# Fillers, halved first weights and a split last product in a recurrent attention and gated FFN kernel

## The chip, the cores and the metric

The kernel runs on one core of a Trainium2 chip. The metric is device time in microseconds (us) of that core, from several executions; lower is better. One further execution was taken by the hardware profiler; its lines are quoted below. In them PE is the matrix engine (PEld its weight loads), DVE the vector engine, ACT the scalar engine, POOL the general engine, and SP the engine that here only issues DMAs. "SPq", "ACTq" and the like are an engine's instruction queue, where DMAs are issued. L394 is line 394 of the kernel.

## The reference

One transformer layer, 2048 tokens of width 640, in bf16. Attention has 32 heads of 128 and is recurrent: it goes through the tokens in 64 segments of 32, and each segment sees 8 memory tokens that are the previous segment's attention output.

```python
for s in range(n_seg):                               # 64 segments, one after the other
    h = concatenate([mem, x[:, s*32:(s+1)*32]])      # 8 memory tokens and 32 tokens
    q, k, v = h @ Wq, h @ Wk, h @ Wv                 # 640 -> 32 heads of 128
    p = softmax(where(mask, q @ k.T * scale, -1e9))
    o = (p @ v) @ Wo                                 # back to 640
    mem = o[:, :8]                                   # what the next segment waits for
    outs.append(o[:, 8:])
```

x is layer-normalized before attention; h = x + attention. After it, for all 2048 tokens: `h2 = h + ((relu(g) * u) @ W_down)` with `g = ln(h) @ W_gate`, `u = ln(h) @ W_up` and 1728 hidden columns.

## The kernel before

The program is written as one list of operations, each with an engine, what it reads and what it writes. `_Graph.solve` turns the keys into semaphore waits, and each engine then runs its operations strictly in the order of the list. DMAs are operations of the engine that issues them (`dma`, L332, on SP unless `eng="act"`); SP's and ACT's DMAs go through two queues. Nothing reorders the list, so the place of a line in the source is its place on its engine.

The work has three stages.

- **Opening** (to about 57 us). SP issues the weights in one row: Wk, Wq and Wv in five pieces of 128 rows each (1 MB a piece, `W[:, j, c, :]`), then Wo in eight pieces. ACT issues two pieces of x (`xt`, `x0`, which borrows the tile oTe) and the first memory (`wtok`). DVE and ACT normalize x, PE transposes it (L360), and then PE makes K and Q of segment 0, of the tokens that are kept for memory use and of the extra tokens (`project`, L394 and L367, three passes per piece). V follows piece by piece (`first_values`). `scores` (L483), exponentials on ACT, masks on DVE, the P·V products (`pv_mem`, L536) and the products with Wo (`wo_pairs`, L599, and `wo_pass`, L582) follow, until `to_act_split` writes the memory rows of segment 1. `keep_busy(n, cols)` (L895) issues 4n products into a bank whose content is not used; it stands in places where PE would otherwise wait.
- **Segments 1 to 63** (to about 826 us). In a loop, PE projects K, Q and V of one segment, and the scores, the P·V products and the products with Wo follow. V is copied into a second layout, VM, by SP's DMAs (`merge_v`); in segment 0 DVE and ACT do this. Toward the end, SP also loads what the FFN needs: `xn2T`, the normalized tokens of the first FFN block, in segment 62, and the gate, up and down weights (`load_piece`, `load_down`).
- **FFN**. Four blocks of 512 tokens: `gate_up` (L858, with the rest of the hidden columns in L871), then `down_pair`: `down_part` multiplies 14 pieces of the hidden columns with W_down into two banks of 320 output columns, `down_out` (DVE, L1133) adds h, `down_store` writes the rows. The very last 128 tokens are done half by half: 14 products of 320 columns, an add, a store, and the same for the other 320 columns.

PE's program is far larger than what the core holds at once: it comes in 16 KB packets through an instruction queue on the same DMA engines (page: 200 packets, 3.28 MB).

Of the kernel before, what the change touches and what calls it, by code (L numbers as in the profile page):

```python
# [27 lines left out]
class _Graph:  # L28
# [10 lines left out]
    def add(self, eng, fn, r=(), w=(), dma=False):  # L39
        if eng == "pool" and not dma:  # L40
            r, w = tuple(r) + (("pool",),), tuple(w) + (("pool",),)
        op = _Op(eng, fn, tuple(r), tuple(w), dma)
        self.ops.append(op)
        return op
# [122 lines left out]
def build_kernel(nc, A_x, A_mem0, A_Wq, A_Wk, A_Wv, A_Wo, A_seg_len, B_W_gate, B_W_up, B_W_down, out):  # L167
# [110 lines left out]
    def B(n):  # L278
        return ("B", n)
# [4 lines left out]
    add("pool", lambda p: p.affine_select(ident[:], ident[:], [[1, 128]], ALU.is_equal, 0.0, base=0,  # L284
                                          channel_multiplier=-1), r=[("ident",)], w=[("ident",)])
    add("pool", lambda p: p.memset(eps[:], 1e-5), w=[("eps",)])
    for i in range(2):
        add("dve", lambda v, i=i: v.memset(oT[i][:], 0.0), w=[("oT", i, n, kh) for n in "mx" for kh in range(2)])
        add("pool", lambda p, i=i: p.memset(act_r[i][:], 0.0),
            w=[("act", i, j, "m") for j in range(4)] + [("act", i, "x")] + [("act", i, "x", j) for j in range(4)])  # L290
        if i == 0:
            add("pool", lambda p: p.memset(ap(Vp, Dh, [[VW, 8], [1, VW - Dh]]), 1.0), w=[("Vp1",)])
        add("pool", lambda p, i=i: p.memset(ap(Ve[i], Dh, [[VW, 8], [1, VW - Dh]]), 1.0), w=[("Ve1", i)])
        add("pool", lambda p, i=i: p.memset(act_e[i][:], 0.0), w=[("acte", i)])
# [30 lines left out]
    def table(a):  # L325
        return a.add_instruction(mybir.InstLoadActFuncSet(name=nc.get_next_instruction_name(), ins=[], outs=[],
                                                          act_func_set_id=6))
    add("act", table)


    def dma(dst, src, r=(), w=(), eng="sp"):
        add(eng, lambda e: e.dma_start(dst, src), r=r, w=w, dma=True)  # L332
# [40 lines left out]
    def project(act, akeys, j, halves, banks, chunks=range(5), ends=(0, DC - 1), held=False, parts=0):  # L373
        swap = 1 if j == 2 and akeys[0][0] == "acte" else 0

        def f(pe):
            left = parts
            for c in chunks:
                for n, i in enumerate(halves):
                    for g in range(4):  # L380
                        o = 2048 * i
                        w = (W[:, j, c, o + 512 * (g ^ swap):o + 512 * (g ^ swap) + 512] if j == 2 else
                             W[:, j, c, o:o + 2048].rearrange("p (h e) -> p h e", e=128)[:, :, 32 * g:32 * g + 32])
                        a = (bank(banks[n])[32 * g:32 * g + 32, :], act[:, c, :], w)
                        if n == 0 and not (held and c == chunks[0]):
                            k = min(left, 2) if c != ends[0] else 0
                            left -= k
                            for q in range(2 if k else 1):
                                b = a if not k else (a[0][:, 256 * q:256 * q + 256], a[1],
                                                     w[:, 256 * q:256 * q + 256] if j == 2 else w[:, 8 * q:8 * q + 8])  # L390
                                if q and k == 1:
                                    ins = again(pe, *b, c == ends[0], c == ends[1], g)
                                else:
                                    ins = pe.matmul(*b, start=(c == ends[0]), stop=(c == ends[1]), skip_group_check=True)  # L394
                        else:
                            ins = again(pe, *a, c == ends[0], c == ends[1], g)
            return ins
        add("pe", f, r=list(akeys) + [("W", j, c) for c in chunks], w=[B(b) for b in banks] + [("Wdone", j)])

    def tok_keys(t):  # L400
        return [("tok", t)] + [("ox", kh, t) for kh in range(2) if t < 2]
# [323 lines left out]


    x0 = oTe[:].rearrange("p h t -> p (h t)")[:, 0:D]
    ln1_load(-1, xt, ("xt",), "act")
    ln1_load(0, x0, ("oTe", 0), "act")
    for g in range(4):  # L730
        dma(wtok[32 * g:32 * g + M, :, :],
            mem0_ap.rearrange("t (c g j) -> g t c j", g=4, j=32)[g], r=[("wtok",)], w=[("wtok0", g)], eng="act")
    srcs = (A_Wq, A_Wk, A_Wv)
    for j in (1, 0, 2):
        for c in range(DC):
            dma(W[:, j, c, :], srcs[j][128 * c:128 * c + 128].rearrange("p h e -> p (h e)"), w=[("W", j, c)])
    for i, lo, hi in [(i, g, g + 1) for i in range(2) for g in range(4)]:
        dma(ap(Wo, (4 * i + 8 * lo) * D, [[8 * D, hi - lo], [1, 4 * D]]),
            A_Wo[16 * i + 4 * lo:16 * i + 4 * hi].rearrange("(g c) (p f) d -> (c p) g (f d)", c=4, f=4), w=[("Wo", i, lo)])
# [159 lines left out]

    scores(0, 0)  # L900
    scores(0, 1)
    first_values((3,))
    keep_busy(20, 32)
    first_values((4,))
    for hf in range(2):
        exp_mem(0, hf)
        mask_mem(0, hf)
# [11 lines left out]
    for a, eng in ((0, "dve"), (1, "act")):  # L919
        (t, ks), flat = v_of(0, a), "p k d -> p (k d)"  # L920
        for x, lo, hi in ((0, 0, 1), (1, 1, 3), (0, 3, 4)):
            x ^= a
            for q in range(lo, hi):
                for k0, k1 in ((0, 4), (4, 8)) if eng == "dve" else ((0, 8),):
                    copy_op(eng, VM[x][32 * q:32 * q + 32, k0:k1].rearrange(flat),
                            t[32 * q:32 * q + 32, k0:k1].rearrange(flat), ks, [("VM", x, q)])
    late_q(1, [("oT", 0, "m", 1)])
    project(xe, xke, 2, (0, 1), BQ, (0, 1))
    for g in range(4):
# [25 lines left out]
    for s in range(1, NSEG):  # L955
# [16 lines left out]
        if s > 0:  # L972
# [29 lines left out]
            else:  # L1002
                norm_x_late(0)
                flip_ox(s - 1, (0,))
            if s == NSEG - 2:
                for n, (lo, hi) in enumerate(((0, 1), (1, 2), (2, 3), (3, DC))):
                    dma(xn2T[0][:, lo:hi, :], xn2_d[:, lo:hi, :], r=[("xn2_d", u) for u in range(4)] + [("Wdone", 0)],
                        w=[("xn2", 0, n)])
            project(a, ks, 2, (0,), (P2,), range(4), held=not last and held[2])
            scores(s, 0, (0, 1))  # L1010
            project(a, ks, 2, (0,), (P2,), (4,))
# [1 line left out]
            if not last:  # L1013
                exp_mem(s, 0)
                first_exp = G.ops[-1]
                mask_mem(s, 0)
            to_v(P2, Vp, 0, ("Vp",), "act")
            if last:
# [80 lines left out]
                r=[("act", p, "x", j), ("act", p, "x"), ("act", *place(s + 1), "m")], w=[("acte", 1 - p)])  # L1099


    def down_part(par, u, bks, js, hfs=(0, 1)):

        def f(pe):
            for j in js:
                p0, p1 = (0, 128) if j < FC - 1 else ((FR, 128) if u % 2 == 0 else (0, FR))
                for hf in hfs:
                    a = (bank(bks[hf])[:, 0:320], hT[par][p0:p1, j, u * 128:(u + 1) * 128],
                         Wd[p0:p1, j, hf * 320:(hf + 1) * 320])
                    if hf == hfs[0] or j == FC - 1:  # L1110
                        i = pe.matmul(*a, start=(j == 0), stop=(j == FC - 1), skip_group_check=True)  # L1111
                    else:
                        i = again(pe, *a, j == 0, j == FC - 1, None)
            return i
        wk = sorted({n for j in js for n in ((j // 3,) if j < FC - 1 else (5, 6))})
        add("pe", f, r=[("hT", par, j) for j in js] + [("Wd", n) for n in wk], w=[B(bks[hf]) for hf in hfs])

    def down_tails(par, u0, bks):

# [9 lines left out]

    def down_out(par, u, bks, o, hfs=(0, 1)):  # L1130
        for hf in hfs:
            bk = bks[hf]
            add("dve", lambda v, hf=hf, bk=bk: v.tensor_tensor(osb[o][:, hf * 320:(hf + 1) * 320], bank(bk)[:, 0:320],  # L1133
                                                               h_rows[par][:, u, hf * 320:(hf + 1) * 320], ALU.add),
                r=[B(bk), ("h", par, u)], w=[("osb", o, hf)])

    def down_store(b, u, o, hfs=(0, 1)):
        t0 = b * TB + u * 128
        lo, hi = 320 * hfs[0], 320 * hfs[-1] + 320
        dma(out_ap[t0:t0 + 128, lo:hi], osb[o][:, lo:hi], r=[("osb", o, hf) for hf in hfs], w=[("out", t0, hfs[0])])  # L1140

    def down_pair(b, n):
        par = b % 2
        s0 = 4 * (par ^ 1 ^ n)
        bks = ((s0, s0 + 1), (s0 + 2, s0 + 3))
        u = 2 * n
        o = [(n_o[0] + q) % 3 for q in range(2)]
        n_o[0] += 2
        final = b == NBLK - 1 and n == 1
        for js in (range(FC - 2), range(FC - 2, FC if final else FC - 1)):  # L1150
            down_part(par, u, bks[0], js)
        if final:
            down_out(par, u, bks[0], o[0])
            down_store(b, u, o[0])
            for hf in range(2):
                down_part(par, u + 1, bks[1], range(FC), (hf,))
                down_out(par, u + 1, bks[1], o[1], (hf,))
                down_store(b, u + 1, o[1], (hf,))
            return
        down_part(par, u + 1, bks[1], range(FC - 1))  # L1160
        down_tails(par, u, bks)
        for q in range(2):
            down_out(par, u + q, bks[q], o[q])
            down_store(b, u + q, o[q])
# [143 lines left out]
```

## Time and profile before

| | |
|---|---|
| median of the runs | 1000.89 us (1000.19, 1000.89, 3407.01) |
| profiled execution | 1000.27 us, span 998.5 us |
| PE, busy share of the span | 97% |
| DVE, ACT, POOL | 72%, 53%, 17% |
| mean granted PE clock | 0.998 |
| DMA, mean over the span | 73 GB/s |
| DMA, 7 to 20 us | 417 GB/s |

The span runs from the first to the last instruction of the profiled execution; the 1.8 us between it and that execution's time lie around it. "Busy" counts instructions in flight, and products overlap, so a busy PE is not PE at its peak. The granted clock is the share of the full PE clock that the chip allowed. A chain of waits follows the work back from the last instruction: at each step to what released it, or to the instruction before it on its engine. A wait for several things is put down to the one that came last.

### The profile page before, as it was taken

Reading aid. Unit: us, or ns where it says so; the run is one execution under the profiler, and the core shown is the slowest. Engines: PE = TensorE matmul, PEld = TensorE weight load, DVE = VectorE, ACT = ScalarE, POOL = GpSimd, SP = SyncE. Lnnn points to the kernel's source line nnn. Section 1 sums busy time; section 2 is a strip of 40 time slices with the busy share of each in tenths; the row PEclk is TensorE's granted clock in tenths of the full one; section 3 lists DMA queues with packets and bytes.
Section 4 is the critical chain, followed back from the end, with each engine's and each line's share of the span. In section 5 each row is a group of like instructions: output and inputs, shape, how many; then the busy total and the mean of one; then the engine's idle time right before and its main releaser. Section 6 shows DMA issues by size and latency. Waiting matters only on the chain.

```text
span 998.5 us, 56385 instructions
## 1 busy us (share of the span) xinstructions
PE 970.3 (97%) x26139; PEld 534.8 (54%) x24878; DVE 715.3 (72%) x1866; ACT 524.4 (53%) x1330; POOL 167.7 (17%) x414
## 2 busy tenths in 40 slices
PE   4789999999999999999999999999999999999998
PEld 1245555555555555555556565655555554344443
DVE  2468787878888887888788878787878766445332
ACT  1456666656666666666666566665656643122120
POOL 7021202021302130222022212121110010000000
PEclk9999999999999999999999999999999999999999
DMA  9930212121222122121212131111111169413100
GB/s 376 415 108 28 54 28 54 30 60 51 54 42 54 48 55 47 48 55 48 50 45 62 46 60 41 41 41 39 41 36 39 36 183 248 99 20 93 27 14 26
DMA packets 73535, 73.34 MB, mean 73 GB/s; under 512 B 42352, under 2 KB 60112, under 8 KB 71376
## 3 DMA queue, kind: packets, MB, share of 16 engines
q1 hardware_dynamic: 71568, 68.83, 24.6%
q8 instruction: 200, 3.28, 1.4%
q10 hardware_dynamic: 1728, 0.91, 0.3%
q14 instruction: 39, 0.32, 0.1%
HBM read 37.04 MB, written 6.55 MB: 44 GB/s over the span
## 4 chain that ended last, share of the span: by engine, by line
PE 93%; SPq 3%; DMA 2%; DVE 1%; ACT 0%; issue 0%; DVEq 0%; ACTq 0%
PE ps L394 47%; PE ps L858 11%; PE ps L367 7%; PE ps L582 7%; PE ps L599 7%; PE ps L642 4%; SPq L332 3%; PE ps L1111 3%; PE ps L483 2%; PE ps L671 2%; DMA Wo<-in_A_Wo_dram 2%; PE ps L536 2%; PE ps L871 0%; PE ps L1124 0%; DVE oT L562 0%
## 5 line engine op out<-in xcount | busy, mean ns | idle before, releaser
L394 PE MATMUL ps<-W,act_r 128*32 128x512 bf16 (+1 forms) x8327 | 453.6, 357 | 1.4 <-DVE act_r L623 0.8
L394 PEld LDWEIGHTS ps<-W,act_r 128*32 128x32 bf16 x8327 | 213.4, 96 | 165.6 <-DVE act_r L623 31.9
L418 ACT ACTIVATE tok<-ps 128x512 bf16<-128x512 f32 x190 | 109.3, 594 | 57.2 <-PE ps L394 48.7
L394 PE MATMUL ps<-W,act_e 128*32 128x512 bf16 x1224 | 119.8, 384 | 7.6 <-DVE TBf L464 3.8
L413 DVE STREAM_TRANSPOSE Ko<-tox 128x512 bf16<-128x512 bf16 x128 | 89.6, 701 | 40.4 <-ACT tox L418 40.1
L491 POOL COPY Qo<-Qe 128x256 bf16<-128x256 bf16 x64 | 28.2, 440 | 527.3 <-DVE oT L556 520.3
L418 ACT ACTIVATE tox<-ps 128x512 bf16<-128x512 f32 x134 | 79.6, 598 | 63.6 <-PE ps L394 43.0
L562 DVE STREAM_TRANSPOSE oT<-tox 128x512 bf16<-128x512 bf16 x128 | 96.6, 755 | 0.0
L413 DVE STREAM_TRANSPOSE Qo<-tok 128x512 bf16<-128x512 bf16 x124 | 85.7, 691 | 0.8
L367 PE MATMUL ps<-W,act_e 128*32 128x512 bf16 x856 | 84.4, 385 | 0.0
L582 PE MATMUL ps<-Wo,oT 128*32 128x160 bf16 x4032 | 81.6, 233 | 1.0 <-DMA Wo<-in_A_Wo_dram 0.9
L599 PE MATMUL ps<-Wo,oT 128*32 128x320 bf16 x2016 | 79.8, 299 | 0.5 <-DVE rm L546 0.5
L582 PEld LDWEIGHTS ps<-Wo,oT 128*32 128x32 bf16 x4032 | 70.5, 97 | 11.1 <-DVE oT L556 3.1
L418 ACT ACTIVATE Vp<-ps 128x512 bf16<-128x512 f32 x127 | 75.2, 592 | 0.5 <-PE ps L858 0.5
L886 ACT ACTIVATE g<-ps 128x512 bf16<-128x512 f32 x52 | 30.1, 593 | 79.3 <-PE ps L858 79.3
L612 ACT ACTIVATE SA<-TA 64x40 f32<-64x40 f32 x126 | 29.5, 234 | 75.3 <-DVE TA L610 74.5
L499 ACT ACTIVATE Pm<-ps 128x64 bf16<-128x64 f32 x126 | 28.1, 223 | 71.8 <-PE ps L483 71.7
L887 DVE TENSOR_TENSOR hT<-g,ps 128x512 bf16<-128x512 bf16 x52 | 35.8, 688 | 40.5 <-PE ps L858 38.6
L858 PE MATMUL ps<-xn2T,Wg 128*128 128x512 bf16 x260 | 64.7, 379 | 0.0
L858 PE MATMUL ps<-xn2T,Wu 128*128 128x512 bf16 x260 | 64.6, 379 | 0.0
L599 PEld LDWEIGHTS ps<-Wo,oT 128*32 128x32 bf16 x2016 | 52.9, 96 | 15.8 <-DVE rm L546 1.2
L556 DVE STREAM_TRANSPOSE oT<-om 128x128 bf16<-128x128 bf16 x126 | 39.0, 309 | 31.0 <-ACT om L548 31.0
(113 smaller groups left out, 1444.5 us busy)
## 6 DMA issues: line engine op xcount, KB each, us to landing
VM<-Vp SPq DMA_DIRECT2D x126, 65.0 KB
VM<-Vp SPq DMA_DIRECT2D x63, 130.0 KB
W<-in_A_Wk_dram SPq DMA_DIRECT2D x5, 1024.0 KB
W<-in_A_Wq_dram SPq DMA_DIRECT2D x5, 1024.0 KB
W<-in_A_Wv_dram SPq DMA_DIRECT2D x5, 1024.0 KB
Wo<-in_A_Wo_dram SPq DMA_DIRECT2D x8, 640.0 KB
attn_d<-wtok SPq DMA_DIRECT2D x248, 7.5 KB
xt<-in_A_x_dram SPq DMA_DIRECT2D x16, 160.0 KB
```

Of the source, the lines that this page charges most:

```text
L367: return pe.add_instruction(mybir.InstMatmult(name=nc.get_next_instruction_name(), engine=mybir.EngineType.PE, ins=[pe.lower_ap(rhs), pe.l ...
L394: ins = pe.matmul(*b, start=(c == ends[0]), stop=(c == ends[1]), skip_group_check=True)
L413: add("dve", lambda v: v.transpose(dst[:, 16 * i:16 * i + 16, 0:32], tok[t][:, :].rearrange("p (h f) -> p h f", f=32)), r=tok_keys(t), w=keys)
L418: add("act", lambda a: a.activation(dst, src, ACTF.Copy), r=r, w=w)
L556: add("dve", lambda v: v.transpose(ap(oT[par], 160 * hf, [[40, 4], [320, 4], [1, 8]]), ap(om, 128 * hf, [[1, 4], [4, 32]])), r=[("om", hf) ...
L562: add("dve", lambda v, kh=kh: v.transpose(ap(oT[p], 160 * kh + M, [[320, 4], [40, 4], [1, 32]]), ap(tox, 128 * kh, [[256, 4], [1, 4], [4, ...
L582: i = pe.matmul(bank(bk)[32 * gg:32 * gg + 32, 0:160], src[:, hb, 0:32], w[:, gg], start=(hb == CH[16 * halves[0]]), stop=(hb == CH[-1]), ...
L599: i = pe.matmul(bank(bk)[32 * q:32 * q + 32, 0:320], src[:, hb, 0:32], w, start=(n == 0), stop=(n == 7), skip_group_check=True)
L642: ins = pe.matmul(bank(bk)[32 * q:32 * q + 32, 0:320], src[:, hb, 0:32], w[:, 2 * (q % 2):2 * (q % 2) + 2], start=(i == 0), stop=(i == 15) ...
L858: ins = pe.matmul(bank(bk), w[:, c, lo:lo + 128], xn2T[par][:, c, :], start=(c == 0), stop=(c == DC - 1))
L886: add("act", lambda a: a.activation(g1[gi][:, :], bank(bg), ACTF.Relu), r=[B(bg)], w=[("g1", gi)])
L887: add("dve", lambda v: v.tensor_tensor(hT[par][:, j, :], g1[gi][:, :], bank(bu), ALU.mult), r=[B(bu), ("g1", gi)], w=[("hT", par, j)])
```

## The change

Seven edits:

1. The tile `oT[1]` is no longer cleared at the start (DVE); `oT[0]` still is.
2. ACT's table load moves from the head of ACT's list to behind its first DMA issues.
3. The first piece of Wk (128 rows) is loaded in two halves: rows 0 to 63 by ACT, ahead of its other DMAs, rows 64 to 127 by SP. The first K products wait for both.
4. Fillers: 12 wide products (512 columns) before V's fourth piece, then 32 narrow ones (32 columns) and 20 wide ones where 80 narrow ones stood, and 16 wide ones after V's fifth piece.
5. In segment 0 DVE copies V into VM in whole rows instead of two halves.
6. The loads of `xn2T` in segment 62 move behind the first exponential of that segment, and wait for it.
7. The last 128 tokens are split into 480 and 160 output columns instead of 320 and 320.

```diff
+    add("dve", lambda v: v.memset(oT[0][:], 0.0), w=[("oT", 0, n, kh) for n in "mx" for kh in range(2)])
     for i in range(2):
-        add("dve", lambda v, i=i: v.memset(oT[i][:], 0.0), w=[("oT", i, n, kh) for n in "mx" for kh in range(2)])
...
-    add("act", table)
...
-        add("pe", f, r=list(akeys) + [("W", j, c) for c in chunks], w=[B(b) for b in banks] + [("Wdone", j)])
+        add("pe", f, r=list(akeys) + [("W", j, c) for c in chunks] + [("W", 1, 0, 0)] * (j == 1 and 0 in chunks), w=[B(b) for b in banks] + [("Wdone", j)])
...
+    dma(W[0:64, 1, 0, :], A_Wk[0:64].rearrange("p h e -> p (h e)"), w=[("W", 1, 0, 0)], eng="act")
     ln1_load(-1, xt, ("xt",), "act")
     ln1_load(0, x0, ("oTe", 0), "act")
...
+    add("act", table)
     srcs = (A_Wq, A_Wk, A_Wv)
     for j in (1, 0, 2):
         for c in range(DC):
-            dma(W[:, j, c, :], srcs[j][128 * c:128 * c + 128].rearrange("p h e -> p (h e)"), w=[("W", j, c)])
+            lo = 64 if (j, c) == (1, 0) else 0
+            dma(W[lo:, j, c, :], srcs[j][128 * c + lo:128 * c + 128].rearrange("p h e -> p (h e)"), w=[("W", j, c)])
...
     scores(0, 0)
     scores(0, 1)
+    keep_busy(3)
     first_values((3,))
-    keep_busy(20, 32)
+    keep_busy(8, 32)
+    keep_busy(5)
     first_values((4,))
+    keep_busy(4)
...
-                for k0, k1 in ((0, 4), (4, 8)) if eng == "dve" else ((0, 8),):
-                    copy_op(eng, VM[x][32 * q:32 * q + 32, k0:k1].rearrange(flat),
-                            t[32 * q:32 * q + 32, k0:k1].rearrange(flat), ks, [("VM", x, q)])
+                copy_op(eng, VM[x][32 * q:32 * q + 32].rearrange(flat), t[32 * q:32 * q + 32].rearrange(flat), ks, [("VM", x, q)])
...
-            if s == NSEG - 2:
-                for n, (lo, hi) in enumerate(((0, 1), (1, 2), (2, 3), (3, DC))):
-                    dma(xn2T[0][:, lo:hi, :], xn2_d[:, lo:hi, :], r=[("xn2_d", u) for u in range(4)] + [("Wdone", 0)],
-                        w=[("xn2", 0, n)])
             project(a, ks, 2, (0,), (P2,), range(4), held=not last and held[2])
             scores(s, 0, (0, 1))
...
                 exp_mem(s, 0)
                 first_exp = G.ops[-1]
+                if s == NSEG - 2:
+                    for n, (lo, hi) in enumerate(((0, 1), (1, 2), (2, 3), (3, DC))):
+                        dma(xn2T[0][:, lo:hi, :], xn2_d[:, lo:hi, :], r=[("xn2_d", u) for u in range(4)] + [("Wdone", 0)],
+                            w=[("xn2", 0, n)])
+                        G.ops[-1].after = first_exp
                 mask_mem(s, 0)
...
+    COLS = ((0, 320), (320, 640), (0, 480), (480, 640))
...
-                    a = (bank(bks[hf])[:, 0:320], hT[par][p0:p1, j, u * 128:(u + 1) * 128],
-                         Wd[p0:p1, j, hf * 320:(hf + 1) * 320])
+                    lo, hi = COLS[hf]
+                    a = (bank(bks[hf % 2])[:, 0:hi - lo], hT[par][p0:p1, j, u * 128:(u + 1) * 128], Wd[p0:p1, j, lo:hi])
...
-            for hf in range(2):
+            for hf in (2, 3):
                 down_part(par, u + 1, bks[1], range(FC), (hf,))
                 down_out(par, u + 1, bks[1], o[1], (hf,))
                 down_store(b, u + 1, o[1], (hf,))
```

The adds and stores of the last rows (`down_out`, `down_store`) take their columns from the same `COLS`.

More of the change, by code (lines that the diff above doesn't have):

```diff
@@ L1115, in down_part @@
         wk = sorted({n for j in js for n in ((j // 3,) if j < FC - 1 else (5, 6))})
-        add("pe", f, r=[("hT", par, j) for j in js] + [("Wd", n) for n in wk], w=[B(bks[hf]) for hf in hfs])
+        add("pe", f, r=[("hT", par, j) for j in js] + [("Wd", n) for n in wk], w=[B(bks[hf % 2]) for hf in hfs])
     def down_tails(par, u0, bks):
@@ L1131, in down_out @@
         for hf in hfs:
[L1132 to L1135, printed above, removed]
+            bk, (lo, hi) = bks[hf % 2], COLS[hf]
+            add("dve", lambda v, lo=lo, hi=hi, bk=bk: v.tensor_tensor(osb[o][:, lo:hi], bank(bk)[:, 0:hi - lo],
+                                                                      h_rows[par][:, u, lo:hi], ALU.add),
+                r=[B(bk), ("h", par, u)], w=[("osb", o, n) for n in {2: (0, 1, 2)}.get(hf, (hf,))])
     def down_store(b, u, o, hfs=(0, 1)):
         t0 = b * TB + u * 128
-        lo, hi = 320 * hfs[0], 320 * hfs[-1] + 320
+        lo, hi = COLS[hfs[0]][0], COLS[hfs[-1]][1]
         dma(out_ap[t0:t0 + 128, lo:hi], osb[o][:, lo:hi], r=[("osb", o, hf) for hf in hfs], w=[("out", t0, hfs[0])])
```

## The prediction

> **What bounds the kernel now.** I read the chain of waits first, as shares, then cut to the opening.
>
> ```profile
> PE 93%; SPq 3%; DMA 2%; DVE 1%; ACT 0%; issue 0%; DVEq 0%; ACTq 0%
> ...
> 33.26 2.13 SPq L332
> 35.43 20.14 DMA Wo<-in_A_Wo_dram
> 55.57 0.04 issue
> 55.61 0.49 PE ps L582 x16
> ```
>
> From 57 us to the end the chain is PE's, with nothing in it that the diff touches before the last products. The first 55.6 us are not PE's: the chain goes through SP's weight issues to the last piece of Wo, landed at 55.57, and the sixteen L582 products that wait for it. Second view, the stages (columns: stretch, its length, busy time of PE, PEld, DVE, ACT, POOL, granted clock, DMA share, GB/s):
>
> ```profile
> 1.80:5.00 3.20, 0.00 (x0) 0.00 (x0) 0.47 (x1) 0.29 (x1) 2.67 (x10) 1.00 0.92 331
> 5.00:20.50 15.50, 5.58 (x54) 1.58 (x34) 5.57 (x23) 0.99 (x4) 11.53 (x59) 1.00 1.02 415
> 34.20:37.60 3.40, 1.05 (x16) 0.21 (x8) 1.37 (x3) 0.11 (x1) 0.00 (x0) 1.00 1.01 419
> 37.60:41.00 3.40, 3.04 (x88) 1.32 (x80) 0.55 (x4) 0.81 (x4) 0.00 (x0) 0.50 1.01 417
> 50.00:53.60 3.60, 3.58 (x88) 1.73 (x72) 0.97 (x3) 2.85 (x6) 0.27 (x1) 1.00 1.01 405
> ```
>
> The DMA engines are full (share 1.0, 405 to 421 GB/s) from 5 us to 53.6. Only the ramp before 5 us is below that. After a stretch in which PE was busy 1.05 of 3.40 us the clock is 0.50, in 37.6 to 41.0 only. Third view, PE in order of time where fillers are changed (start, length, what, idle before it and who ended that):
>
> ```profile
> 40.39 0.62 PE L394 MATMUL ps<-W,act_e 128*32 128x512 bf16 x4
> ...
> 41.57 0.52 PE L895 MATMUL ps<-W,act_e 128*32 128x32 bf16 x48
> 43.80 0.38 PE L895 MATMUL ps<-W,act_e 128*32 128x32 bf16 x32 [1.71 <-issue]
> 44.00 0.42 PE L394 MATMUL ps<-W,act_e 128*32 128x512 bf16 x4
> ...
> 45.90 0.24 PE L536 MATMUL ps<-Ve,Pbd 128*32 128x129 bf16 x4 [0.83 <-ACT Vp L418]
> ```
>
> After 48 of 80 narrow fillers PE stands 1.71 us and nothing in the profile ends it. The DMA view of 41 to 42 us shows one 16 KB packet of the instruction queue: I take 43.80 as a border, where the next block of PE's program had to arrive through the full DMA engines.
>
> **The change, part by part.** The profiled execution took 1000.27 us (span 998.5, 1.77 around it); the median shown is 1000.89, the lowest run 1000.19. My sum is against 1000.27.
>
> First weights in halves. Bytes are the same, so only the ramp can give. SP's first issue takes 0.39 us for 128 rows. Two halves issued side by side put descriptors before all engines in about half that: I take 0.2 us. Bounds: nothing; and the whole ramp, (415-331) x 3.2 / 415 = 0.65 us. I take the lower part because only the issue is halved, not the first reads. The ACT queue now carries 0.5 MB ahead of xt, oTe and wtok: 1.3 us later at 415 GB/s, 2.5 at half of it. wtok sets PE's start (L394 waits until 17.05), so the K products start 1.3 to 2.5 us later, and may pay one more half-clock window (3.4 us of work at half pace, 1.7). PE is idle 0.94, 1.35 and 1.43 us for the three V pieces at 33.02, 35.42 and 37.91, 3.7 in all, which takes up what I expect: cost 0. Without that cover it is paid one for one. The new wait, K's first product on the second half, has all of PE behind it. That product began at 12.18, and the half is due near 5 us.
>
> Table load after the issues: six ACT issues end at 5.5 us, seven near 6.1, plus 1.28 of loading gives 7.4 against the first ACTIVATE at 7.20. 0.2 us on the x rows, which wait for wtok anyway: 0. One memset less (0.59 on DVE, which then waits 3.78 for xt): 0. Whole VM copies on DVE instead of eight halves (306 ns each, 2.4 in all; four whole ones cost between 1.2 and 2.4): DVE waits for L599 afterwards, so 0.
>
> Fillers. Count stays 80, so the border stays at the same instruction, but now 12 wide products stand before V's piece 3, then 32 narrow and some 4 wide reach the border, and 16 wide follow it; 16 more stand after piece 4. A wide one costs 54 ns (sixteen from 48.24 to 49.10), double at half clock. Piece 3 was ready at 40.39; twelve from 40.33, half of them slow, end near 41.3, so it ends near 42.2, still before the border. If the block again arrives for 43.80, 16 wide take 0.86 and piece 4 starts at 44.66 instead of 44.00: 0.66 late. The last 16 (0.86) lie under the 1.2 us before the P·V products (0.83 of it idle). So the P·V products and everything behind them come 0.66 late. Cover: PE's waits for Wo before 52.47, 54.04 and 55.61. After the preceding fillers' last issue they are 0.17, 0.63 and 0.63, 1.43 in all. Cost 0, with 0.77 left. Bounds: 0 (nothing in front of 55.61 can gain, Wo lands when it lands) and, beyond the cover, one for one; no row shows a border with another order in front.
>
> xn2T loads (L332, segment 62). Four issues, 2.04 us from 798.34, now wait for the first exp (ACT 798.96, 0.22 long), so start 0.9 us later. Behind them on SP are the three VM pieces (issued from 801.00, now about 801.3) and two weight pieces (803.23). VM is read at 807.18, four us after its last issue; xn2T and the weights at 810.02. Cost 0. Without the cover PE waits one for one.
>
> The end. Groups by shape (busy us, mean ns of one | idle before):
>
> ```profile
> L871 PE MATMUL ps<-xn2T,Wt 128*128 128x256 bf16 x40 | 5.0, 272 | 0.0
> ...
> L360 PE MATMUL ps<-ident,xt 64*128 64x64 bf16 x5 | 0.4, 235 | 8.3 <-DVE xt L350 8.3
> ...
> L627 DVE TENSOR_TENSOR fold<-ps,fold 128x160 f32<-128x160 f32 x1 | 0.3, 318 | 0.0
> ```
>
> And the last add in order of time:
>
> ```profile
> 995.43 0.49 DVE L1133 TENSOR_TENSOR osb<-ps,h 128x320 bf16<-128x320 f32 x1 [1.62 <-PE ps L1111]
> ```
>
> The chain gives 0.136 us per 320-column product, 0.217 per 512 (L858, 90 in 19.53) and 0.109 per 256 (L871, 10 in 1.09): 0.42 ns a column. 480 columns then cost 0.203 and 160 cost 0.069; 14 x (0.203+0.069) = 3.81 = 28 x 0.136. PE: 0, if loading 128 columns of weights hides under 0.069. L360 says so: five in 0.44 with 0.235 each, 0.05 apart at the cold start, weights loaded between. Bound above: no narrower product at full clock than L871's, 14 x (0.109-0.069) = 0.56. [...] The last add shrinks from 0.49 to the 0.32 of L627's 160 columns: -0.17. The store's payload halves: 40 KB less at 415 GB/s is at most 0.1, not counted.
>
> Sum: -0.2 - 0.17 = -0.37, so 999.9.
>
> **Rivals.**
>
> No gain in the opening: the two halves share the same full engines, and the stream's end is set by its slowest engine. For: the DMA share is 0.92 already in 1.8 to 5.0. Then only -0.17 is left: 1000.1. [...]
>
> Slower: PE arrives late at the last piece of Wo (55.61). It decides where the delay of V's piece 4 passes 1.43 us. If the wider fillers delay the border block too (0.98, what stands before piece 3) and the 16 wide behind it run in a half-clock window (another 0.86), the delay is 0.66+0.98+0.86 = 2.5, less 1.43 = +1.07, with the end's -0.17: 1001.2. For: the block's fetch began at 41.4, just as piece 3 was issued. Against: the border is counted in instructions, and 24 of them moved ahead of it.
>
> The narrow last pass is load-bound: 14 x 0.04 = +0.56, with the rest of the sum 1000.4.
>
> Faster: the whole ramp of 0.65 is won, with -0.17: 999.4.
>
> **How the numbers follow.** Forecast 0.40, no gain in the opening 0.25, slower 0.12, load-bound end 0.10, whole ramp 0.11, something not seen here 0.02. The likeliest gives 999.9. The range is 998.9 to 1001.2: below, the whole ramp (999.4) less half of the 0.7 between the median and the lowest run and the store's 0.1; above, the slower case, which also holds the forecast if the run falls like 1000.89. Two per cent is 20 us, about what a measurement here tells from no change; no case moves over 1.1 us, so within 0.98 and 0.01 on either side for the unseen.
>
> **What would show it.** The last Wo landing near 55.4 and the last L582 group waiting for it (right), or that group following the filler before it without a wait (slower rival). First V piece still started by its DMA. A gap behind 36 fillers after piece 3, then 16 wide, piece 4 near 44.7. Products of the last pass 0.07 apart (right) or 0.11 (load-bound). Last add near 0.32. No PE wait at 807 or 810. A time off by more than 1.1 us would mean that a cause outside these rows acts.

## The result and the profile after

| | before | after |
|---|---|---|
| median of 12 runs | 1000.89 us | 1003.38 us |
| lowest run | 1000.11 us | 1002.51 us |
| profiled execution | 1000.27 us, span 998.5 us | 1004.5 us, span 1002.5 us |
| last piece of Wo landed | 55.57 us | 57.83 us |
| last group of products that needs it | 55.61 us | 59.04 us |

After is 2.5 us slower by the medians; the ratio of the runs is 1.0028, with a 95% interval of 1.002 to 1.0036. One run of before took 3407.01 us, for a reason that nothing here shows; it does not move the median. The profiled execution of after is one of its longer ones, 4.0 us over before in span. Line numbers have moved: L394 is now L392, L367 is L365, L895 is L896, L582 is L580, L536 is L534, L1111 is L1116, L1133 is L1138, and the DMA helper L332 is L330.

First the chain of waits of the kernel after, as shares and then cut to the opening (start, length, what):

```profile
PE 94%; DMA 3%; DVE 1%; SPq 1%; issue 1%; ACT 0%; DVEq 0%; ACTq 0%
```

```profile
11.79 30.96 DMA W<-in_A_Wv_dram
42.80 0.40 PE ps L392 x4
...
44.29 2.16 issue
46.45 1.05 PE ps L896 x16
...
49.12 1.71 PE ps L896 x16
```

SP's share fell from 3% to 1%. Before, the chain stayed with the weight stream until the last piece of Wo at 55.57. Now it leaves the stream with V's fourth piece at 42.80 and goes on through PE: a stand of 2.16 us and two groups of wide fillers. So there are two things to explain: why V's fourth piece is at 42.80 instead of 40.39, and why PE is behind Wo afterwards.

For the first, the stages in the first 9 us (columns: stretch, its length, busy time of PE, PEld, DVE, ACT, POOL, granted clock, DMA share, GB/s), of before:

```profile
1.80:4.00 2.20, 0.00 (x0) 0.00 (x0) 0.47 (x1) 0.29 (x1) 1.86 (x7) 1.00 0.93 309
4.00:6.50 2.50, 0.00 (x0) 0.00 (x0) 0.45 (x2) 0.00 (x0) 1.91 (x9) 1.00 1.01 393
6.50:9.00 2.50, 0.44 (x5) 0.28 (x5) 1.26 (x6) 0.50 (x2) 1.88 (x10) 1.00 1.02 411
```

and of after:

```profile
1.80:4.00 2.20, 0.00 (x0) 0.00 (x0) 0.00 (x0) 0.00 (x0) 1.85 (x7) 1.00 0.88 238
4.00:6.50 2.50, 0.00 (x0) 0.00 (x0) 0.00 (x0) 0.00 (x0) 1.91 (x9) 1.00 1.02 220
6.50:9.00 2.50, 0.00 (x0) 0.00 (x0) 0.00 (x0) 1.28 (x1) 1.88 (x10) 1.00 0.94 254
```

The next-to-last column says that the DMA engines are nearly as busy as before. The last says that they move 56 to 77% as much. The packets of the weights are 8 KB in both; between 4 and 6.5 us their median time is 312 ns before and 602 ns after. The share of busy time alone would have hidden this: from 4 to 6.5 us a share of 1.02 went with 220 GB/s, where one of 1.01 went with 393. The halves landed one after the other, SP's at 6.07 and ACT's at 8.90; the whole piece had landed at 5.71. Every later piece of the weights landed later than before too, by 1.6 to 3.1 us, most of them by 2.3 to 2.5.

For the second, PE in order of time (start, length, what, idle before it and who ended that), after:

```profile
42.80 0.40 PE L392 MATMUL ps<-W,act_e 128*32 128x512 bf16 x4 [0.26 <-DMA W<-in_A_Wv_dram]
...
43.67 0.62 PE L896 MATMUL ps<-W,act_e 128*32 128x32 bf16 x36
46.45 1.05 PE L896 MATMUL ps<-W,act_e 128*32 128x512 bf16 x16 [2.16 <-issue]
47.33 0.51 PE L392 MATMUL ps<-W,act_e 128*32 128x512 bf16 x4
...
48.89 1.93 PE L896 MATMUL ps<-W,act_e 128*32 128x512 bf16 x16
50.60 0.34 PE L534 MATMUL ps<-Ve,Pbd 128*32 128x129 bf16 x4
...
59.04 0.46 PE L580 MATMUL ps<-Wo,oT 128*32 128x160 bf16 x16
```

and the stages around it:

```profile
44.10:47.50 3.40, 1.24 (x24) 0.44 (x20) 0.00 (x0) 0.00 (x0) 0.00 (x0) 1.00 1.03 415
47.50:50.90 3.40, 3.40 (x45) 1.33 (x36) 1.72 (x3) 1.19 (x2) 0.00 (x0) 0.50 1.02 413
```

The border stands behind 36 fillers, as forecast, but 2.16 us long. After it the granted clock is 0.50 for 3.4 us, and the second sixteen wide fillers take 1.93 us instead of 1.05. The last L580 group starts without a wait, 1.21 us after its Wo landed; before it started 0.04 us after. So at 59 us after is 3.43 us behind: 2.26 by the stream, 1.17 by PE. By the end of the segments it is 4.18: 0.33 more within the next 12 us, 0.51 more around the moved loads of segment 62, and 0.09 regained between them. The end gives 0.17 back: 4.0.

The end, in order of time:

```profile
998.32 1.10 PEld L1116 LDWEIGHTS ps<-Wd,hT 128*128 128x128 bf16 x14 [0.21 <-issue]
998.42 0.66 DVE L1138 TENSOR_TENSOR osb<-ps,h 128x480 bf16<-128x480 f32 x1 [2.15 <-PE ps L1116]
999.60 0.32 DVE L1138 TENSOR_TENSOR osb<-ps,h 128x160 bf16<-128x160 f32 x1 [0.52 <-PE ps L1116]
```

The last add takes 0.32 instead of 0.49. Fourteen weight loads of the narrow pass fit into 1.10 us, 0.08 apart, and the last thirty products take 4.61 us in the chain of waits of both kernels.

### The profile page after: what moved, and what is told of

Read it like the earlier page. It is cut to its first block, busy times and chain, and to the rows that moved or that the text cites. A ratio compares the mean times of both kernels' runs of the same rounds, so it can differ in the third digit from the quotient of the medians.

```text
span 1002.5 us, 56373 instructions
## 1 busy us (share of the span) xinstructions
PE 971.7 (97%) x26125; PEld 536.1 (53%) x24878; DVE 713.9 (71%) x1861; ACT 524.5 (52%) x1330; POOL 167.4 (17%) x414
## 4 chain that ended last, share of the span: by engine, by line
PE 94%; DMA 3%; DVE 1%; SPq 1%; issue 1%; ACT 0%; DVEq 0%; ACTq 0%
PE ps L392 47%; PE ps L859 11%; PE ps L365 7%; PE ps L580 7%; PE ps L597 7%; PE ps L640 4%; PE ps L1116 3%; DMA W<-in_A_Wv_dram 3%; PE ps L481 2%; PE ps L669 2%; PE ps L534 2%; SPq L330 1%; PE ps L896 1%; PE ps L872 0%; PE ps L1129 0%
## 5 line engine op out<-in xcount | busy, mean ns | idle before, releaser
L392 PE MATMUL ps<-W,act_r 128*32 128x512 bf16 (+1 forms) x8327 | 453.7, 357 | 2.2 <-ACT tok L416 1.2
L392 PEld LDWEIGHTS ps<-W,act_r 128*32 128x32 bf16 x8327 | 213.3, 96 | 167.4 <-DVE act_r L621 32.1
L392 PE MATMUL ps<-W,act_e 128*32 128x512 bf16 x1224 | 119.6, 383 | 3.9 <-DVE TBf L462 3.6
L365 PE MATMUL ps<-W,act_e 128*32 128x512 bf16 x856 | 84.5, 386 | 0.0
L580 PE MATMUL ps<-Wo,oT 128*32 128x160 bf16 x4032 | 81.4, 233 | 0.2 <-DVE oT L554 0.2
L580 PEld LDWEIGHTS ps<-Wo,oT 128*32 128x32 bf16 x4032 | 70.8, 97 | 9.5 <-DVE oT L554 3.5
L859 PE MATMUL ps<-xn2T,Wg 128*128 128x512 bf16 x247 | 61.8, 379 | 1.3 <-issue 1.0
L554 DVE STREAM_TRANSPOSE oT<-om 128x128 bf16<-128x128 bf16 x126 | 39.0, 309 | 31.5 <-ACT om L546 31.4
```

The costliest lines, as they stand in the source:

```text
L365: return pe.add_instruction(mybir.InstMatmult(name=nc.get_next_instruction_name(), engine=mybir.EngineType.PE, ins=[pe.lower_ap(rhs), pe.l ...
L554: add("dve", lambda v: v.transpose(ap(oT[par], 160 * hf, [[40, 4], [320, 4], [1, 8]]), ap(om, 128 * hf, [[1, 4], [4, 32]])), r=[("om", hf) ...
L580: i = pe.matmul(bank(bk)[32 * gg:32 * gg + 32, 0:160], src[:, hb, 0:32], w[:, gg], start=(hb == CH[16 * halves[0]]), stop=(hb == CH[-1]), ...
L859: ins = pe.matmul(bank(bk), w[:, c, lo:lo + 128], xn2T[par][:, c, :], start=(c == 0), stop=(c == DC - 1))
```

## The experiments

Each was timed against runs of the kernel before on the same chip (medians 1000.61 to 1000.73), unless it says one execution. "Shift" is the time after minus before, by the profiles, at which the first products with VM start (59.10 us in before), the first group behind the opening that is the same in all.

### Each suspect alone

**Edit 3 alone**, put into before:

```diff
+    dma(W[0:64, 1, 0, :], A_Wk[0:64].rearrange(...), w=[("W", 1, 0, 0)], eng="act")
...
+            lo = 64 if (j, c) == (1, 0) else 0
-            dma(W[:, j, c, :], srcs[j][128 * c:128 * c + 128]...)
+            dma(W[lo:, j, c, :], srcs[j][128 * c + lo:128 * c + 128]...)
```

> The kernel before with edit 3 alone (first Wk piece in row halves from ACT's and SP's queue). Theory 'stream': the halves move at 220 to 240 GB/s instead of 415, all later pieces land 2.2 to 2.6 us later (last Wo piece at about 57.9 instead of 55.57), and the time rises by 2.0 to 2.6 us. Rival 'fillers': the stream's loss hides under PE's waits, the time rises by under 0.7 us.

Measured: 1002.96 us, ratio 1.0023 (1.0014 to 1.0031). The stages and the last group of products:

```profile
4.00:6.50 2.50, 0.00 (x0) 0.00 (x0) 0.00 (x0) 0.00 (x0) 1.91 (x9) 1.00 0.97 210
```

```profile
58.66 0.46 PE L582 MATMUL ps<-Wo,oT 128*32 128x160 bf16 x16
```

Wo's last piece landed at 57.98. This edit alone carries the slow rate and 2.2 of the 2.5 us. Here too PE is 0.68 late at Wo, with the old fillers, in a half-clock window from 46.99 to 53.82.

**After without edit 3** (the piece in one DMA again, everything else as changed):

```diff
-    dma(W[0:64, 1, 0, :], A_Wk[0:64].rearrange(...), w=[("W", 1, 0, 0)], eng="act")
...
-            dma(W[lo:, j, c, :], srcs[j][128 * c + lo:128 * c + 128]...)
+            dma(W[:, j, c, :], srcs[j][128 * c:128 * c + 128]...)
```

> The changed kernel with edit 3 undone, all else kept. Theory 'stream': the last Wo piece lands near 55.5 again; left are +0.5 from the moved xn2T loads, -0.2 at the end and at most 0.5 from the fillers: 0 to +0.8 us against before. Rival 'fillers': most of the loss stays, +2 us or more.

Measured: 1000.36 us, ratio 0.9998 (0.9989 to 1.0007). In order of time:

```profile
44.06 1.05 PE L894 MATMUL ps<-W,act_e 128*32 128x512 bf16 x16 [1.85 <-issue]
...
55.78 0.46 PE L580 MATMUL ps<-Wo,oT 128*32 128x160 bf16 x16 [0.44 <-DMA Wo<-in_A_Wo_dram]
```

With the piece whole again, the loss is gone, and the wait for Wo is back in its old place.

**The fillers alone**, edit 4 put into before:

```diff
+    keep_busy(3)
     first_values((3,))
-    keep_busy(20, 32)
+    keep_busy(8, 32)
+    keep_busy(5)
     first_values((4,))
+    keep_busy(4)
```

> The kernel before with edit 4 alone (the fillers). Theory 'stream': V's last piece starts 0.5 to 0.8 us later, the last Wo products still wait for their DMA at 55.6, time within 0.4 us of before. Rival 'fillers': the last Wo products start without a wait, 1 to 2 us late, and the time rises by as much.

Measured: 1000.49 us, ratio 0.9997 (0.9988 to 1.0006), shift 0.0.

```profile
44.06 1.05 PE L895 MATMUL ps<-W,act_e 128*32 128x512 bf16 x16 [1.28 <-issue]
...
55.61 0.46 PE L582 MATMUL ps<-Wo,oT 128*32 128x160 bf16 x16 [0.30 <-DMA Wo<-in_A_Wo_dram]
```

The block behind the border came 0.26 later than in before (44.06 for 43.80). V's last piece started at 44.92, 0.92 later, a little more than expected (0.5 to 0.8), and the P·V products 0.91 later. All of it was taken up ahead of Wo: 0.30 of wait is left.

**After with the old fillers** (the last diff reversed):

> The changed kernel with the fillers of before. Theory 'stream': the last Wo products wait for their DMA near 57.9; time against before +2.3 to +2.9 (stream 2.3, moved loads 0.5, end -0.2), so 0 to 1.2 us below the changed kernel, whose PE came 1.2 us after the landing. Rival 'fillers': within 0.7 us of before.

Measured: 1003.13 us, ratio 1.0023 (1.0014 to 1.0033). The border takes 2.87 us here, Wo lands at 58.17, and the last L580 group starts at 58.22. So the fillers are not the cause of the loss. Against their own runs of before the two kernels lose 2.49 us with the new fillers and 2.40 with the old ones; the difference is too small to be told here.

### What about the halves is slow

**Rows 0 to 63 and 64 to 127, both from SP's queue**, in before:

```diff
-            dma(W[:, j, c, :], srcs[j][128 * c:128 * c + 128]...)
+            for lo, hi in (((0, 64), (64, 128)) if (j, c) == (1, 0) else ((0, 128),)):
+                dma(W[lo:hi, j, c, :], srcs[j][128 * c + lo:128 * c + hi]...)
```

> The kernel before, first Wk piece as two DMAs of 64 rows, both on SP's queue. Theory 'half the rows': a transfer that goes to 64 of the 128 partitions moves at half rate whatever its queue; 8 KB packets near 600 ns instead of 309 until about 6 us, last Wo piece near 57.8, time +2 us or more. Rival 'two queues': alternating between two queues is what costs; packets stay at 309 ns, time within 0.7 us of before.

Measured: 1003.1 us, ratio 1.0024 (1.0015 to 1.0033), last Wo at 57.43.

```profile
4.00:6.50 2.50, 0.00 (x0) 0.00 (x0) 0.70 (x2) 0.00 (x0) 1.91 (x9) 1.00 1.01 211
```

One queue is as slow (211 GB/s). The second queue is not the cause.

**Two halves by columns**, 128 rows of 4 KB each, from ACT and SP:

```diff
+    dma(W[:, 1, 0, 0:2048], A_Wk[0:128, 0:16].rearrange(...), w=[("W", 1, 0, 0)], eng="act")
...
+            lo = 16 if (j, c) == (1, 0) else 0
+            dma(W[:, j, c, 128 * lo:], srcs[j][128 * c:128 * c + 128, lo:]...)
```

> The kernel before, first Wk piece as two DMAs of 128 rows and half the columns each, from ACT's and SP's queue. Theory 'half the rows': full rate, last Wo piece at 55.3 to 55.9, time within 0.5 us of before, though x lands later. Rival 'two queues': as slow as row halves, last Wo near 57.9, +2 us.

Measured: 1000.94 us, ratio 1.0002 (0.9994 to 1.0011), last Wo at 55.67.

```profile
4.00:6.50 2.50, 0.00 (x0) 0.00 (x0) 0.00 (x0) 0.00 (x0) 1.91 (x9) 1.00 1.03 419
```

Halves from two queues that span all rows moved at 419 GB/s from 4 to 6.5 us (393 in before), and gained nothing.

**Even rows from ACT, odd rows from SP**, 64 rows each:

```diff
+    dma(W[0:128:2, 1, 0, :], A_Wk[0:128:2].rearrange(...), w=[("W", 1, 0, 0)], eng="act")
...
+                dma(W[1:128:2, j, c, :], srcs[j][1:128:2]...)
```

> The kernel before, first Wk piece as two DMAs of 64 rows, even rows from ACT's queue and odd rows from SP's. If one side of the partitions being idle is what costs, this spreads over both sides and runs at full rate: last Wo near 55.6, time within 0.5 us. If the number of rows (64 instead of 128) costs, or the two queues do, +2 us as with the row halves.

Measured: 1001.01 us, ratio 1.0003 (0.9994 to 1.0012), last Wo at 55.54.

```profile
4.00:6.50 2.50, 0.00 (x0) 0.00 (x0) 0.00 (x0) 0.00 (x0) 1.91 (x9) 1.00 0.95 392
```

So it is not the number of rows either: two times 64 rows, each spread over alternate partitions, moved at 392 GB/s. Its profile has a half-clock window from 44.04 to 50.87 and a shift of 0.92; the times, 0.4 us over before, neither show that much nor exclude it.

**Destination and source apart.** In the last runs the rows read and the partitions written changed together. Two kernels change only one of them; both use SP's queue. In both, Wk's first 128 rows stand in another order in W, and K is computed from that. The first reads alternate rows and writes neighbouring partitions:

```diff
+            if (j, c) == (1, 0):
+                for n in range(2):
+                    dma(W[64 * n:64 * n + 64, 1, 0, :], A_Wk[n:128:2].rearrange(...), ...)
+                continue
```

> Before, with the first Wk piece as two transfers from SP's queue: rows 0, 2, 4 .. 126 of Wk's first 128 go to partitions 0 to 63, rows 1, 3 .. 127 to partitions 64 to 127. So Wk's first 128 rows stand in another order and K is computed from that; every byte and every product is there. If the range of SBUF partitions written decides the rate: as slow as the row halves from one queue (239, 211, 306 GB/s in 1.8 to 4, 4 to 6.5 and 6.5 to 9 us), 8 KB packets 550 to 600 ns, last Wo at 57.4 +- 0.4, 1002.8 to 1003.4 us. If the contiguous 512 KB read from memory decides: 272, 392, 391 GB/s as in the even and odd rows, packets near 309 ns, last Wo at 55.6 +- 0.2, 1000.3 to 1001.2 us.

One execution: 1003.09 us (before beside it 1001.05), last Wo at 57.90, 8 KB packets 607 ns from 4 to 6.5 us.

```profile
4.00:6.50 2.50, 0.00 (x0) 0.00 (x0) 0.14 (x1) 0.00 (x0) 1.91 (x9) 1.00 1.03 218
```

The second reads neighbouring rows and writes alternate partitions:

```diff
+                    dma(W[n:128:2, 1, 0, :], A_Wk[64 * n:64 * n + 64].rearrange(...), ...)
```

> The reverse: rows 0 to 63 of Wk (one contiguous 512 KB) go to partitions 0, 2, 4 .. 126, rows 64 to 127 to partitions 1, 3 .. 127, both from SP's queue. Wk's first 128 rows again stand in another order. If the partitions written decide: full rate, near 390 GB/s in 4 to 6.5 us, packets near 309 ns, last Wo at 55.6 +- 0.2, 1000.3 to 1001.2 us. If the contiguous half read decides: near 211 GB/s in 4 to 6.5 us, last Wo at 57.4 +- 0.4, 1002.8 to 1003.4 us. If both this one and the one before are slow or both fast, neither theory holds alone.

One execution: 1001.12 us (before beside it 1001.05), last Wo at 56.36, packets 347 ns.

```profile
4.00:6.50 2.50, 0.00 (x0) 0.00 (x0) 0.88 (x2) 0.00 (x0) 1.90 (x10) 1.00 1.00 326
```

The partitions written decide most of it, by one execution each: neighbouring partitions were slow whichever rows were read (218 GB/s with alternate rows, 211 with neighbouring ones), and alternate partitions (326 GB/s) lost 0.8 us of stream instead of 2.3. Those 0.8 were not expected (55.6 was), are more than the scatter (with this piece in one DMA the last Wo landed at 55.55 to 55.82 in five profiles), and are not explained.

**The dose.** The first three Wk pieces, each as two row halves from SP:

```diff
+            for lo, hi in (((0, 64), (64, 128)) if j == 1 and c < 3 else ((0, 128),)):
```

> The kernel before, the first three Wk pieces as two DMAs of 64 rows each, all on SP's queue. Theory 'half the rows': every piece adds what one adds, some 1.9 us on the stream (e5: last Wo 57.43 against 55.57), so last Wo near 61.1 and time about +5.6 to +6.5 us. Rival: the cost is that of the start alone (the first packets), and the time is that of e5, +2.5 us.

Measured: 1008.67 us, ratio 1.0079 (1.0065 to 1.0092), 8.1 us. The last Wo landed at 62.95, 7.38 later than before, and PE waited for it.

```profile
4.00:6.50 2.50, 0.00 (x0) 0.00 (x0) 0.00 (x0) 0.00 (x0) 1.91 (x9) 1.00 1.03 217
...
12.00:14.50 2.50, 0.00 (x0) 0.00 (x0) 1.14 (x4) 0.50 (x2) 1.89 (x10) 1.00 1.00 214
```

```profile
62.99 0.46 PE L582 MATMUL ps<-Wo,oT 128*32 128x160 bf16 x16 [0.28 <-DMA Wo<-in_A_Wo_dram]
```

The cost comes with every piece and is not one of the start. It is 2.5 us a piece, more than the 1.9 that were expected; the rate stayed between 213 and 230 GB/s from 4 to 14.5 us.

### The moved loads, and the rest

**Edit 6 alone**, in before: the four `xn2T` loads behind segment 62's first exponential (the diff is in the change above).

> The kernel before with edit 6 alone (xn2T loads behind the first exponential of segment 62). Theory: 0, PE's P.V products of segment 62 and the first gate products not later than before by more than 0.1 us. Rival: SP's later issues delay VM and the gate weights, 0.3 and 0.2 us as in the profile of the changed kernel, +0.5 us.

Measured: 1000.86 us, ratio 1.0001 (0.9992 to 1.001). The time shows nothing; the profile shows 0.3 us between segments 61 and 63, and where it comes from:

```profile
807.61 0.59 PE L671 MATMUL ps<-VM,Px 64*32 64x129 bf16 x32 [0.16 <-DMA VM<-Vp]
```

The last VM piece landed at 807.52, and the products that read it start 0.09 us later; so do they in after (811.10 and 811.19). In before it landed at 804.62 and was read at 807.18, so 2.56 us of cover are gone. SP's part is seen in order of time (start, length of the issues, what), in before:

```profile
798.34 2.04 SPq L332 DMA_DIRECT2D xn2T<-xn_d  x4
801.00 2.18 SPq L332 DMA_DIRECT2D VM<-Vp  x3
```

and in after:

```profile
802.93 2.89 SPq L330 DMA_DIRECT2D xn2T<-xn_d  x4
805.86 0.51 SPq L330 DMA_DIRECT2D VM<-Vp  x1
```

Four issues took 2.89 us instead of 2.04, one of them alone 1.54. In both kernels VM's pieces stand and land behind the 640 KB of `xn2T` (808.42 and 811.10; before 803.8 and 804.62). But in before SP stood still for 0.62 us between the two groups, and the last VM piece took 2.03 us from its issue to its landing; in after the groups follow without a break, and it took 4.05 (3.66 with edit 6 alone).

**After without edits 3, 4 and 6** (the diffs above reversed):

> The changed kernel without edits 3, 4 and 6: left are the 480 and 160 columns at the end and the small DVE and ACT edits. Theory: -0.2 us in the span (last add 0.17 shorter), which is under what the timed runs resolve: ratio 0.999 to 1.0005. Rival: the small edits hide a cost of their own, +0.5 us or more.

Measured: 1000.31 us, ratio 0.9997 (0.9988 to 1.0006). Its profile is 0.28 us ahead of before at the last products and 0.53 at the end of the span (998.0). In the times this is not told from no change. So this kernel is faster than after, and not shown to be faster than before.

**After with halves by columns** (the columns diff in after):

> The changed kernel with the first piece halved by columns instead of by rows, two queues as in the change. Theory: the whole loss of the changed kernel is in the row halves, so it comes back to -0.2 to +0.5 us against before. Rival: the fillers and the second queue together keep 1 us or more of it.

Measured: 1001.39 us, ratio 1.001 (1.0001 to 1.0019), 0.8 us. That lies between the two theories, and the interval, 0.1 to 1.9 us, takes in both. Last Wo landed at 55.52, and the shift is -0.05, so the stream's loss is gone. In the profile 0.34 us appear within the next 12 us and 0.56 around the moved loads. The first of the two is in all four profiles of kernels that have edit 3, by rows or columns, together with the small DVE and ACT edits, and in none of the others; 0.23 of it is a wait of PE for DVE's `oT` (L554). Why the two together do this was not tried and stays open.

**After once more**, for the PE part of the loss, one execution:

> The changed kernel once more, for one profile. [...]

Measured: 1002.52 us, last Wo at 57.83 as in the first profile.

```profile
46.46 1.05 PE L896 MATMUL ps<-W,act_e 128*32 128x512 bf16 x16 [2.31 <-issue]
...
48.20 1.04 PE L896 MATMUL ps<-W,act_e 128*32 128x512 bf16 x16
...
57.87 0.46 PE L580 MATMUL ps<-Wo,oT 128*32 128x160 bf16 x16 [0.17 <-DMA Wo<-in_A_Wo_dram]
```

The same kernel with the same border, but the clock stayed at 1.0: the second group of wide fillers takes 1.04 and not 1.93, and PE waits for Wo again. The shift is 2.26, Wo's lateness alone. So the 1.17 us of PE in the first profile are a half-clock window that one execution has and another has not. The twelve runs of after bear this out: the three with a mean clock of 0.998 have spans of 1002.3 to 1002.5 us, the two with 0.999 and the seven with 1.000 spans of 1000.6 to 1002.0. The median run is thus one without the full lateness, and its 2.5 us are in the main the stream's 2.3.

## Why the prediction was wrong

**The first weights in halves: here it failed.** The step was "Bytes are the same, so only the ramp can give", with the bounds "nothing; and the whole ramp", and 0.2 us taken as a gain. The bytes are the same, but the rate is not: a row half writes 64 neighbouring partitions, and such a transfer moved at 210 to 220 GB/s with the engines' busy share at 0.97 to 1.03. The 1.05 MB of the piece take 1.05 / 0.220 = 4.77 us at after's rate and 1.05 / 0.415 = 2.53 at the rate of the opening. The difference, 2.24, is nearly the 2.26 by which Wo landed late. It is paid in full because the prediction's first reading was right: the opening is bound by the stream.

The 0.2 us of gain is not there either. The prediction had half the rows issued in half the time. SP's issue of 64 rows took 0.59 us and ACT's 0.63, where the issue of all 128 rows took 0.39, and the first 8 KB packet started at 2.18 instead of 1.86. The even and odd rows have this too (0.60 and 0.61, first packet at 2.18) and landed Wo on time, so it is not what costs the 2.3.

The bounds were closed on the loss side without a row. No DMA in before's opening wrote 64 partitions with rows of this size, so the rate of one was a price that the trace did not show. It had to be bounded from both sides, or the "two halves side by side" to be made a rival with half the rate of the opening, which by the arithmetic above is 1.05 / 0.2075 - 2.53 = 2.53 us, near the 2.5 that were measured.

The runs agree with each other: 210, 211, 218 and 220 GB/s for neighbouring partitions, 392 for alternate ones from two queues, 419 for halves by columns. Why neighbouring partitions were slower no run shows. The first rival, no gain in the opening, is what the halves by columns gave (ratio 1.0002); for the halves by rows it was wrong too: 1.0023 from two queues, 1.0024 from one.

**The K products' start and its cover.** Forecast 1.3 to 2.5 us later; it was 4.8. These are the products behind `wtok`, in before:

```profile
17.05 0.62 PE L394 MATMUL ps<-W,act_e 128*32 128x512 bf16 x4 [3.82 <-DVE TBf L464]
```

in after:

```profile
21.87 0.62 PE L392 MATMUL ps<-W,act_e 128*32 128x512 bf16 x4 [3.64 <-DVE TBf L462]
```

and in before with halves by columns:

```profile
18.81 0.62 PE L394 MATMUL ps<-W,act_e 128*32 128x512 bf16 x4 [3.41 <-DVE TBf L464]
```

By columns, at full rate, the lateness is 1.8 and inside the forecast. In after ACT's other loads stood behind a half that was itself slow. The cover held all the same: V's waits of 3.7 us, and the stream's own 2.3 on top of them, left 0.26 of wait at V's fourth piece. The first three V pieces no longer wait for their DMA, where the prediction expected the first still to do so.

**The slower rival.** It had a late PE at the last Wo piece through the fillers, the border and a half-clock window. Its parts are in the first profile (border 2.16, wide fillers 1.93, 1.17 late at Wo), and the second profile of the same kernel has none of the lateness. Its price was near (1.07 beyond the cover, 1.17 measured), but it is not the cause of the loss: without the halves the fillers cost nothing (shift 0.0, wait for Wo 0.30).

**Fillers.** The order behind the border (36 fillers, then sixteen wide) and the cover of 1.43 were right; the 0.66 of delay was 0.92 where the fillers ran alone. In after P·V came 4.7 late and the last Wo group 3.43: 1.3 were taken up.

**Table load, memset, VM copies.** Forecast 0. None was run alone; after without edits 3, 4 and 6 still has them, and is not slower.

**The moved loads.** Forecast 0 because VM was read four us after its last issue. What counted was its landing. The loads stood ahead of VM before the edit too; what they lost is their head start, so that VM's pieces were issued while those bytes were still on the way. Around segment 62 this costs 0 to 0.6 us by the profiles and is not told from 0 by the times.

**The end.** Right: PE 0 (4.61 us both times), last add 0.32, 0.17 won. The load-bound rival fell: its 0.56 us was an estimate from L871's wider products, and no run shows it. A load of 128 columns took 0.098 us and overlapped with the next, so the narrow pass's loads are 0.08 us apart.

## What to carry to other kernels

If a DMA is cut at all (the cut by columns gained nothing either), cut it along its bytes and not along its partitions: 64 neighbouring partitions moved at 210 to 220 GB/s where 128 moved at 393 to 419, while the engines' busy share was 0.97 to 1.03 in both cases. When DMA engines look full, read GB/s and the time of a packet beside the share. And where a transfer is moved in a queue, ask which bytes are still on the way when the one that is waited for is issued, and not only when that issue comes.

## What was not expected of the hardware

- The border in PE's program took between 1.28 and 2.87 us in the runs in which it shows, with nothing else in the profile to wait for. It was 1.71 in before. The DMA engines were full: 413 GB/s from 41 to 42 us in before, 415 at a share of 1.03 from 44.1 to 47.5 in after. A 16 KB packet of the instruction queue starts just ahead of it (41.41 in before, 44.13 in after, 1.0 and 1.1 us long). That PE waits for this packet is argued from that and not shown by a run of its own; nor does a run show how much of its program the core holds at once, only that in before 24 or 25 packets of this queue come in every 100 us from 100 to 800 us.
- The clock was halved in one execution and not in another: two profiles of one kernel, with gaps of 2.16 and 2.31 us at the same place, had one a window at 0.50 from 47.5 to 50.9 and the other none. What decides it was not tried.
- Neighbouring rows read into alternate partitions from one queue (326 GB/s, 0.8 us of stream) were slower than alternate rows into alternate partitions from two queues (392 GB/s, no loss). Queue and source differ between the two, so the cause stays open.
- Single DMA issues on SP took 1.4 to 1.8 us around segment 62, where most take 0.3 to 0.7. One of 1.68 is in before too, so the edit is not the cause.
